# Attention and two MLPs on one core: the first stage in another order

## The chip, the core and the metric

The kernel runs on one core of a Trainium2 chip. The metric is the device time of one execution in microseconds (us), as a median of several. In the profile PE is TensorE's matmul, PEld its weight load, DVE is VectorE, ACT ScalarE, POOL GpSimd and SP the engine that issues most DMAs.

## What is computed

Inputs q, k, v have 4 batches, 8 heads, 576 positions and 64 columns per head. The attention is the sum of a pooled one (positions averaged by four, 144 of them, the result repeated four times) and a local one (each position sees those less than four away). Two MLPs follow on the 2304 tokens of 512 features, with 2048 inner features each:

```python
out_up = np.repeat(sm_attn(q_d, k_d, v_d), factor, axis=2)      # pooled by factor = 4
scores = np.where(np.abs(pos[:, None] - pos[None, :]) < factor, scale * q @ k^T, -1e9)
x = out_up + softmax(scores) @ v
h = x @ w_in;  x = (h - np.tanh(h)) @ w_out
h = x @ w_in2; x = (h * np.cos(h)) @ w_out2
```

## The kernel before

All MLP products are made of three products of operands split in a high and a low part (`xh`, `xl` and the like), so each weight tile of 128 inner features has to be split on the chip too. A weight tile goes through four steps of the class `Weights`: `load` (a DMA into one of two raw slots, in this stage), `begin` (two ScalarE instructions), `mid` (one on VectorE, then one cast, on GpSimd for the first three tiles and on ScalarE for the rest) and `end` (one subtraction on GpSimd). `tick` does a mid, a load, a begin and an end at once.

**First stage** (`first_attention`). The first 512 positions of batch 0 are handled on PE, as dense products. The stage is a list of steps, each with a key; the list is sorted by key and issued in that order. Every engine works through its own instructions in that order, and waits where an operand or a buffer isn't ready. So the keys set the order on each engine, and nothing else does. The steps:

- `load_nat`, `load_lo`, `load_vg`, `load_vl`, `load_vw`: loads of q and k by 128 positions, of the left-over 64 positions of the four batches, of v in pooled order, and of v in eight windows of 70 positions. All go through SP's queue. q, k and `vw` tiles share 12 buffers.
- `tr`, `tr_l`: transposes of a q or k tile on PE, copied out by ScalarE (q) or VectorE (k).
- `red_k`, `red_q`, `pooled_k`, `pooled_q`: sums by four; `pooled_q` also calls `left_q`, eight small GpSimd copies out of `klq`.
- `P.s`, `P.e`, `P.n`, `P.t`, `P.t2`, `P.v` for each of four head pairs: the pooled attention. Scores on PE and their maximum on VectorE, exponentials on ScalarE, the division on GpSimd, transposes on PE, value products on PE. `vsum` sums v by four on GpSimd for them.
- `b_s`, `b_m`, `b_n`, `b_t` for each of eight blocks of 64 positions: the local attention. Scores on PE (tile `cs`, three PSUM buffers), maximum and subtraction on VectorE and exponentials on ScalarE, the division on VectorE, transposes on PE copied by ScalarE (`cp`).
- `b_v`, `b_l` for each of four pairs of blocks: 32 value products on PE (`pa_o`), the addition of the pooled part on VectorE, the copy to `xh` on ScalarE; then `xl` by VectorE.

After each step of `tr`, `tr_l`, `b_s`, `b_t` and `b_v`, `at_time` puts one empty product on PE, `idle<-zero`, whose result is never read; `masks` puts ten at the start:

```python
def at_time(t, fn, *a):
    def run():
        fn(*a)
        if fn in with_pe:
            warm(1)
```

At keys from 26.5 on, `early` loads eight tiles of q, k and v for the first unit of the next part (1.7 MB), and from 27.19 on three ticks prepare the first weight tiles. Two raw slots are filled before, at 23.6.

**Then the planner** (`Plan`). The first MLP (`ffn1`, five chunks of tokens, four of them planned) runs on PE. Meanwhile GpSimd and VectorE do the local attention of the other batches in seven units of 128 rows: for each head a product `prod_s` or `prod_v` on GpSimd and a reduction on VectorE; three of the units also do the pooled attention of their batch on PE, for which `psum_qk` and `psum_v` sum by four on VectorE. A step has an engine, an assumed duration, a due time and what it waits for; the planner picks the order of all engines from these before the launch. A group of `ffn1` is 12 products per half into one of two PSUM buffers `h`, then tanh (ScalarE), subtraction (VectorE), copy `gh` (ScalarE) and `gl` (VectorE). The first two groups of chunk 0 are cut into token halves of 256, so that their first half can run before the last quarters of x exist. They have all their steps in the plan. After the planned part come the last chunk and the second MLP, which the change doesn't touch.

## Time and profile before

| | us |
|---|---|
| median of 3 runs (889.93 to 891.58) | 890.36 |
| the profiled execution's own time | 890.26 |
| its span, first to last instruction | 888.5 |
| PE busy | 871.6 |
| VectorE busy | 574.0 |
| ScalarE busy | 473.1 |
| GpSimd busy | 398.0 |

All times in the trace count from the first instruction. A row of the order of time gives start, length, engine, line and operation, and in brackets how long the engine stood idle before and what released it. Busy time of PE has all its products in it, the empty ones too. The first stage ends near 48 us.

### The profile page before, as it was taken

How to read it: one execution, taken by the hardware profiler on the slowest of the kernel's cores; microseconds unless marked ns; L12 is line 12 of the kernel's file. 1: busy time of each engine (PE TensorE's matmuls, PEld its weight loads, DVE VectorE, ACT ScalarE, POOL GpSimd, SP SyncE). 2: the span in 40 equal slices, each digit the busy share in tenths (PEclk: the TensorE clock that was granted, in tenths of full speed). 3: DMA queues.
4: the chain of work that ended last, by engine and by line, in shares of the span. 5: the costliest groups of instructions: out<-in, count | busy, mean ns of one | idle time of the engine just before them, and what ended most of it. 6: DMA issues, size and time to landing. Idle time of an engine off the chain costs nothing.

```text
span 888.5 us, 13043 instructions
## 1 busy us (share of the span) xinstructions
PE 871.6 (98%) x4648; PEld 722.9 (81%) x4648; DVE 574.0 (65%) x953; ACT 473.1 (53%) x967; POOL 398.0 (45%) x406
## 2 busy tenths in 40 slices
PE   8989999999999999999999999999999999999997
PEld 5677877998887888888888888888888888888896
DVE  5788978889988876554453676364546553655454
ACT  4778887354235432554674776354535543544454
POOL 7489999988978778410441232011101110111110
PEclk9999999999999999999999999999999999999999
DMA  9687745545434342532442131011001100000100
GB/s 213 202 266 264 252 154 175 179 128 161 137 106 130 103 152 81 185 111 95 142 143 72 72 102 41 0 48 48 1 1 47 48 1 24 24 25 1 36 13 24
DMA packets 72323, 89.03 MB, mean 100 GB/s; under 512 B 22720, under 2 KB 48326, under 8 KB 72258
## 3 DMA queue, kind: packets, MB, share of 16 engines
q1 hardware_dynamic: 70882, 83.22, 30.5%
q0 software_dynamic: 1232, 4.72, 1.6%
q8 instruction: 36, 0.59, 0.3%
q14 instruction: 29, 0.24, 0.1%
q10 hardware_dynamic: 144, 0.26, 0.1%
HBM read 78.74 MB, written 9.44 MB: 99 GB/s over the span
## 4 chain that ended last, share of the span: by engine, by line
PE 85%; POOL 5%; DMA 3%; issue 2%; ACT 2%; DVE 1%; SPq 1%; POOLq 0%; ACTq 0%; DVEq 0%
PE h L1082 39%; PE oacc L1354 22%; PE acc L1108 19%; POOL pr L869 2%; POOL pr L820 1%; DMA kt<-in_k_dram 1%; POOL i L251 1%; SPq L607 1%; POOL o L251 1%; PE pa_x L1019 1%; PE pa_s L491 1%; DMA lpt<-in_v_dram 1%; PE pa_t L525 0%; DMA raw<-in_moe_w_in_dram 0%; DMA raw<-in_moe_w_out_dram 0%
## 5 line engine op out<-in xcount | busy, mean ns | idle before, releaser
L1354 PE MATMUL oacc<-o,i 128*128 128x512 f32 x864 | 207.8, 390 | 0.0
L1082 PE MATMUL h<-xh,i 128*128 128x512 f32 (+1 forms) x656 | 197.4, 369 | 2.8 <-DVE gl L1131 2.2
L1369 POOL TENSOR_SCALAR y<-y 128x512 f32<-128x512 f32 (+1 forms) x80 | 46.0, 575 | 343.4 <-ACT y L1367 330.0
L1108 PE MATMUL acc<-gh,o 128*128 128x512 f32 (+1 forms) x640 | 194.3, 372 | 1.6 <-POOL o L251 1.6
L1082 PE MATMUL h<-x2h,i 128*128 128x512 f32 (+1 forms) x640 | 191.9, 368 | 0.0
L1354 PEld LDWEIGHTS oacc<-o,i 128*128 128x128 f32 x864 | 161.3, 188 | 33.2 <-ACT i L1095 0.4
L1082 PEld LDWEIGHTS h<-xh,i 128*128 128x128 f32 x656 | 118.6, 189 | 22.7 <-issue 3.0
L1108 PEld LDWEIGHTS acc<-gh,o 128*128 128x128 f32 x640 | 116.4, 189 | 22.7 <-POOL o L251 2.7
L1082 PEld LDWEIGHTS h<-x2h,i 128*128 128x128 f32 x640 | 117.0, 188 | 20.4
L820 POOL TENSOR_TENSOR pr<-qt,kt 128x896 f32<-128x896 f32 x56 | 118.8, 2132 | 14.8 <-DMA kt<-in_k_dram 6.9
L1082 PE MATMUL h<-xl,i 128*128 128x512 f32 (+1 forms) x328 | 119.4, 365 | 0.8 <-DVE xl L1034 0.4
L1108 PE MATMUL acc<-gl,o 128*128 128x512 f32 (+1 forms) x320 | 118.0, 369 | 0.0
L1082 PE MATMUL h<-x2l,i 128*128 128x512 f32 (+1 forms) x320 | 117.9, 368 | 0.0
L869 POOL TENSOR_TENSOR pr<-vt,s 128x896 f32<-128x896 f32 x56 | 105.8, 1945 | 9.5 <-DMA vt<-in_v_dram 4.8
L1374 DVE TENSOR_TENSOR h<-h,rr 128x512 f32<-128x512 f32 (+1 forms) x80 | 51.6, 645 | 80.5 <-ACT rr L1373 80.4
L1372 ACT ACTIVATE rr<-rr 128x512 f32<-128x512 f32 (+1 forms) x80 | 47.1, 588 | 98.3 <-DVE rr L1371 98.0
L1099 ACT ACTIVATE gh<-h 128x512 fp32r<-128x512 f32 x72 | 42.9, 596 | 75.5 <-PE acc L1108 50.1
L1376 DVE TENSOR_TENSOR i<-h,i 128x512 fp32r<-128x512 f32 (+1 forms) x80 | 50.7, 634 | 44.6 <-ACT i L1095 44.5
L1367 ACT ACTIVATE y<-h 128x512 f32<-128x512 f32 (+1 forms) x80 | 44.2, 552 | 60.0 <-PE h L1082 60.0
L1370 DVE TENSOR_TENSOR rr<-y,h 128x512 f32<-128x512 f32 (+1 forms) x80 | 50.3, 628 | 32.6 <-POOL y L1369 32.6
L1082 PEld LDWEIGHTS h<-xl,i 128*128 128x128 f32 x328 | 62.0, 189 | 10.2 <-DVE xl L1034 0.6
L825 DVE TENSOR_REDUCE s<-pr 128x14 f32<-128x896 f32 x56 | 60.3, 1078 | 14.4 <-POOL pr L820 14.2
(205 smaller groups left out, 1208.3 us busy)
## 6 DMA issues: line engine op xcount, KB each, us to landing
raw<-in_moe_w_in_dram SPq DMA_DIRECT2D x32, 512.0 KB, 6.5
raw<-in_moe_w_out_dram SPq DMA_DIRECT2D x32, 512.0 KB, 4.1
kt<-in_k_dram SPq DMA_DIRECT2D x48, 256.0 KB, 3.6
vt<-in_v_dram SPq DMA_DIRECT2D x48, 256.0 KB, 2.7
x2d<-xs SPq DMA_DIRECT2D x8, 512.0 KB, 2.9
x2l<-x2d POOLq DMA_DIRECT2D x4, 1024.0 KB, 5.6
out_dram<-os SPq DMA_DIRECT2D x15, 256.0 KB, 3.5
qt<-in_q_dram SPq DMA_DIRECT2D x24, 128.0 KB, 2.2
```

Source lines behind the costliest of these rows:

```text
L820: nc.gpsimd.tensor_tensor(out=pr.rearrange("p j f d -> p j (f d)"), in0=view(L["q", h], [[0, OFF], [1, 2 * D]], off=f * D), in1=view(L["k" ...
L825: nc.vector.tensor_reduce(out=L["s", u // 2][:, 2 * (u % 2) + e], in_=pr, axis=AX.X, op=ALU.add)
L869: nc.gpsimd.tensor_tensor(out=pr.rearrange("p f d j -> p j f d"), in0=view(L["v", h], [[D, OFF], [D, 2], [1, D]], off=f * D), in1=view(L[" ...
L1082: nc.tensor.matmul(hp[:, cs], lhsT=wt[:, kk * 128:(kk + 1) * 128], rhs=xt, start=(kk + c == 0), stop=(kk == KD - 1 and c == 2))
L1108: nc.tensor.matmul(acc[e], lhsT=wt[:, e * 128:(e + 1) * 128], rhs=gt, start=(f == 0 and i == 0), stop=(f == KF - 1 and i == 2))
L1354: nc.tensor.matmul(acc[t], lhsT=gt[:, t * 128:(t + 1) * 128], rhs=wt, start=(g == 0 and a_ == 0), stop=(g == KF - 1 and a_ == 2))
L1367: iy = nc.scalar.activation(y, hp, AF.Copy, scale=INV_TWO_PI, bias=ROUND)
L1369: ip = nc.gpsimd.tensor_scalar(out=y, in0=y, scalar1=-ROUND, scalar2=-TWO_PI_HI, op0=ALU.add, op1=ALU.mult)
L1370: nc.vector.tensor_tensor(out=r, in0=y, in1=hp, op=ALU.add)
L1372: nc.scalar.activation(r, r, AF.Abs)
L1374: nc.vector.tensor_tensor(out=hp, in0=hp, in1=r, op=ALU.mult)
L1376: nc.vector.tensor_tensor(out=G[f][1], in0=hp, in1=G[f][0].bitcast(F32), op=ALU.subtract)
```

## The change

The first stage has the same steps with other keys. An empty product follows a step only where its key is below 14. The three ticks are gone; load, begin, mid and end of the weights are steps of the stage with keys of their own. The first token halves of the first two MLP groups are steps too (`half`), and the plan takes these groups up at their second half. The eight early loads stand at 9.45 instead of 26.5. In the planned part ten products of the values are made by ScalarE (`prod_v_scalar`, 14 instructions each, `SCALAR` by unit and head), and the sums by four of seven entries are made by GpSimd with two additions, in place in the loaded tile (`sum_4`, `SUMS` by batch, kind and head; kind 0 has two sums, kind 1 one). The planner's constants and the engines' assumed first free times are other ones.

```diff
 
 
-LATENCY, SLACK, STICK = 0.08, 0.16, 0.17
+LATENCY, SLACK, STICK = 0.07, 0.16, 0.31
 
 
...
-                if fn in with_pe:
+                if fn in with_pe and t < WARM:
                     warm(1)
...
@@ -632,7 +652,24 @@
             G["vl"] = lo_load(v)
 
         def load_w():
-            W1.load(raw_a, 2)
+            W1.load(raw_a)
+
+        def begin_w():
+            assert W1.begun < W1.loaded
+            W1.begin()
+
+        def mid_w():
+            assert W1.mids < W1.begun
+            W1.mid()
+
+        def end_w():
+            assert W1.done < W1.mids
+            W1.end(nc.gpsimd)
+
+        def half(j):
+            assert W1.done > j and G["l", 0] and G["l", 1] and len(halves) == j
+            halves.append(group(ch, j, (j,), GS, False))
+            next(halves[j])
...
         with_pe = (tr, tr_l, b_s, b_t, b_v)
-        keyed = [(-9.08, masks), (-2.95, load_vl), (-1.21, load_vg), (13.94, pooled_k), (14.57, pooled_q), (23.6, load_w)]
+        keyed = [(-65.35, masks), (-0.93, load_vl), (4.13, load_vg), (12.99, pooled_k), (14.20, pooled_q)]
         for fn, nm, ts in (
-                (load_nat, "k", (-27.24, -17.23, -14.7, -18.39)),
-                (load_nat, "q", (-24.75, -9.9, -12.13, -14.48)),
-                (tr, "k", (-7.7, -9.06, -1.75, -9.05)),
-                (tr, "q", (-9.07, 12.44, 4.09, 7.14)),
-                (load_lo, "k", (-6.53, 7.68)),
-                (load_lo, "q", (-16.92, -1)),
-                (tr_l, "k", (13.83, 20)),
-                (tr_l, "q", (12.23, 25.24)),
+                (load_nat, "k", (-41.22, -26.44, -22.97, -34.25)),
+                (load_nat, "q", (-27.49, -14.70, -22.30, -19.81)),
+                (tr, "k", (-32.58, -17.04, 1.62, -33.53)),
+                (tr, "q", (-22.03, 8.94, 3.57, 4.78)),
+                (load_lo, "k", (-2.97, 6.88)),
+                (load_lo, "q", (-18.37, -1)),
+                (tr_l, "k", (10.88, 20)),
+                (tr_l, "q", (8.59, 16.86)),
         ):
             keyed += [(t, (fn, nm, i)) for i, t in enumerate(ts)]
         for fn, ts in (
-                (red_k, (3.96, 7.32, -1.37, 2.46)),
-                (red_q, (5.59, 12.45, 9.08, 8.75)),
-                (load_vw, (10.75, 7.88, 12.18, 3.99, -3.26, 8.66, 1.31, 0.91)),
-                (whole(P.s), (15.59, 16.13, 19.35, 18.35)),
-                (whole(P.e), (17.02, 18.39, 19.82, 19.23)),
-                (whole(P.n), (17.03, 18.4, 20.33, 21.49)),
-                (whole(P.t), (18.41, 21.2, 20.87, 25.75)),
-                (whole(P.t2), (19.25, 21.21, 23.95, 25.76)),
-                (whole(P.v), (20, 23.87, 27.22, 27.25)),
-                (b_s, (2.86, 14, 16.37, 16.46, 13.52, 20.14, 20.68, 19.06)),
-                (b_m, (12.2, 15, 17.07, 19.28, 13.53, 20.15, 23.21, 24.99)),
-                (b_n, (12.22, 17.81, 18.06, 19.36, 13.86, 20.16, 26.33, 25.07)),
-                (b_t, (13.87, 18.43, 19.97, 27.23, 17.92, 25.52, 28.49, 30.08)),
-                (b_v, (27.86, 28.36, 30.02, 31.66)),
-                (b_l, (31.35, 30.05, 30.42, 38.71)),
+                (red_k, (4.20, 8.14, 11.73, -7.26)),
+                (red_q, (-1.07, 11.04, 5.06, 9.35)),
+                (load_vw, (10.81, 2.62, 19.18, 8.20, 20.46, 22.38, 4.81, 17.90)),
+                (whole(P.s), (15.22, 15.48, 19.48, 17.29)),
+                (whole(P.e), (16.50, 17.34, 19.95, 18.80)),
+                (whole(P.n), (16.75, 17.40, 21.98, 19.76)),
+                (whole(P.t), (18.08, 20.01, 23.16, 20.48)),
+                (whole(P.t2), (18.94, 21.41, 24.52, 20.49)),
+                (whole(P.v), (20, 23.44, 25.49, 26.30)),
+                (b_s, (-10.60, 14, 16.51, 17.22, 5.89, 19.74, 20.17, 19.33)),
+                (b_m, (5.97, 15, 16.91, 19.12, 8.20, 22.99, 24.29, 20.71)),
+                (b_n, (9.30, 17.07, 18.48, 19.49, 10.42, 24.88, 27.74, 25.47)),
+                (b_t, (14.56, 19.45, 24.84, 26.21, 16.74, 27.43, 31.08, 31.66)),
+                (b_v, (28.50, 28.82, 36.30, 37.40)),
+                (b_l, (29.88, 34.47, 53.77, 56.00)),
         ):
             keyed += [(t, (fn, i)) for i, t in enumerate(ts)]
-        for nm, o_, ts in (("vg", vd, (17.17, 19.17, 20.37, 21.31)), ("vl", vl, (16.11, 20.3, 15.05, 14.86))):
+        for fn, ts in (
+                (load_w, (31.37, 7.62, 29.89, 10.27, 42.57)),
+                (begin_w, (24.69, 25.47, 30.70, 31.76)),
+                (mid_w, (26.53, 28.40, 36.10)),
+                (end_w, (26.60, 35.69)),
+        ):
+            keyed += [(t + 0.001 * i, fn) for i, t in enumerate(ts)]
+        keyed += [(t, (half, j)) for j, t in enumerate((36.45, 54.89))]
+        for nm, o_, ts in (("vg", vd, (16.95, 20.01, 21.04, 25.11)), ("vl", vl, (16.90, 22.74, 15.13, 26.28))):
             keyed += [(t, (vsum, o_, nm, u)) for u, t in enumerate(ts)]
         for t, fn in keyed:
             at_time(t, *(fn if isinstance(fn, tuple) else (fn,)))
         ch.x = None
...
+
+    def sum_cost(*a):
+        return ("POOL", 0.65) if a in SUMS else ("DVE", 0.56)
...
+        def prod_v_scalar(u, e):
+            h = 2 * u + e
+            if e == 0:
+                L["o", u] = ao.tile([128, 2, 2, D], F32, tag="o", name="o", bufs=10)
+            pr = at.tile([128, 2, D, OFF], F32, tag="pr", name="pr", bufs=2)
+            seen["v", u, e] = pr
+            s = L["s", u // 2].rearrange("p q j f -> p (q j f)")
+            for f in range(nf):
+                for j in range(OFF):
+                    i = ((2 * (u % 2) + e) * OFF + j) * nf + f
+                    nc.scalar.activation(pr[:, f, :, j], L["v", h][:, f + j, :], AF.Copy, scale=s[:, i:i + 1])
+                yield
+
...
+        def sum_4(o, t, off):
+            nc.gpsimd.tensor_tensor(out=t[:, off:off + 2, :], in0=t[:, off:off + 2, :], in1=t[:, off + 2:off + 4, :], op=ALU.add)
+            nc.gpsimd.tensor_tensor(out=o, in0=t[:, off, :], in1=t[:, off + 1, :], op=ALU.add)
...
+            if (b, 0, h) in SUMS:
+                sum_4(t[:, 0, e, :], L["q", h], 0)
+                yield
+                sum_4(t[:, 1, e, :], L["k", h], R - 1)
+                return
...
+                    if (ch.i, h) in SCALAR:
+                        p_ = plan.chain(prod_v_scalar(u, e), t, [("ACT", 0.8, dict(new=new, use=[name("v", h), s_, name("o", u)])),
+                                                                 ("ACT", 0.8, dict(use=[name("v", h), s_, pr, name("o", u)]))],
+                                        after=lds + out["soft", u // 2], prev=p_)[-1]
+                    else:
+                        p_ = plan.add("POOL", 1.97, t, lambda u=u, e=e: seen.__setitem__(("v", u, e), (prod_v(u, e, 0), L["prod"])[1]),
+                                      after=lds + out["soft", u // 2], prev=p_, new=new, use=[name("v", h), s_, name("o", u)])
...
-    TL = 26.5
-    HALVES, XLAST, RAWLAST = 2, 0.51, 3.90
-    TPGAP, TPS = 13.96, -2.17
-    REDLATE, LOADEARLY, FINEARLY, WLOAD = -6.92, 31.46, 7.92, 25.27
+    TL = 9.45
+    HALVES, XLAST, RAWLAST = 2, 5.76, 3.99
+    TPGAP, TPS = 14.11, -3.58
+    REDLATE, LOADEARLY, FINEARLY, WLOAD = -4.57, 13.51, 10.16, 18.40
     NORM = "A"
     WIDE = (), (2,), (2,), (2,)
-    WEARLY, URGENT = 50.47, 90.64
-    LENGTHS = 98.20, 59.66, 106.15, 108.05
-    SPANS = (-14.12, 71.46), (62.49, 107.38), (105., 143.), (157.39, 185.), (205.13, 257.46), (238.36, 274.93), (250.07, 330.89)
+    WEARLY, URGENT = 51.07, 123.07
+    LENGTHS = 98.26, 60.50, 113.62, 107.25
+    SPANS = (-14.69, 69.93), (71.07, 107.38), (105., 143.), (174.03, 185.), (215.87, 259.12), (236.67, 273.73), (257.96, 311.03)
     PRIO = 200
+    FREE = 1.18, 4.20, 4.00, 3.01
+    ACTV = "00000000010000000010010000011010000110011000000000000000"
+    SCALAR = [(i // 8, i % 8) for i, c in enumerate(ACTV) if c == "1"]
+    SUMBITS = "000000001000000001000000000000100000000010011001"
+    SUMS = [(1 + i // 16, i // 8 % 2, i % 8) for i, c in enumerate(SUMBITS) if c == "1"]
     AHEAD = 100.00
     LAG = 3
-    TE, TD, KE = 27.19, 1.82, 3
     NE, NG, NEARLY = 6, 3, 3
     rw = w2e = xb = W2 = None
     events = []
     exps = []
+    WARM = 14.00
+    halves, GS = [], {}
...
                     t = begin + 0.1 * j
-                c = plan.chain(group(ch, j, fs, G, j in WIDE[ci]), t, [
+                begun = ci == 0 and j < HALVES
+                c = plan.chain(halves[j] if begun else group(ch, j, fs, G, j in WIDE[ci]), t, [
                     ("PE", mm / 2, dict(new=[("ps_a" if j in WIDE[ci] else "ps_h", h)], use=[x], after=ready[:2 * per] + [wready.get(("i", f)) for f in fs])),
...
                 done[j] = c[-1]
-                firsts.append(c[1])
+                firsts.append(c[1 - begun])
...
-    events += [(TE + TD * i, 0, lambda: W1.tick(raw_a, nc.gpsimd)) for i in range(KE)]
...
-                dict(x=["x0"], raw=["raw3", "raw4"], wf=["wf1", "wf2", "wf3"]), dict(PE=0.0, ACT=0.5, DVE=1.5, POOL=1.0, SP=0.0))
+                dict(x=["x0"], ps_h=[f"h0.{j}" for j in range(HALVES)], raw=["raw3", "raw4"], wf=["wf1", "wf2", "wf3"]), dict(zip(("PE", "ACT", "DVE", "POOL"), FREE), SP=0.0))
```

By the new keys PE's steps come in this order: `tr` k 3, k 0, q 0, k 1; `b_s` 0; `tr` k 2, q 2, q 3; `b_s` 4; `tr_l` q 0; `tr` q 1; `tr_l` k 0; `b_s` 1; `b_t` 0; `P.s` 0, 1; `b_s` 2; `b_t` 4; `tr_l` q 1; `b_s` 3; `P.s` 3; `P.t` 0; `P.t2` 0; `b_s` 7; `b_t` 1; `P.s` 2; `b_s` 5; `tr_l` k 1; `P.v` 0; `P.t` 1; `b_s` 6; `P.t` 3; `P.t2` 3, 1; `P.t` 2; `P.v` 1; `P.t2` 2; `b_t` 2; `P.v` 2; `b_t` 3; `P.v` 3; `b_t` 5; `b_v` 0, 1; `b_t` 6, 7; `b_v` 2; `half` 0; `b_v` 3; `half` 1. SP's are: k 3 loads ahead of q 0, both left-over q loads and one of k, `vl`, `vw` 1, `vg`, `vw` 6, the last left-over k, one weight tile, `vw` 3, the eight early tiles, a second weight tile, `vw` 0, 7, 2, 4, 5, and the other three weight tiles as their slots come free.

## Rows read from the trace of the kernel before

**Rows 1.** The page: its head, and busy time with share and instructions of each engine.

```profile
span 888.5 us, 13043 instructions
...
PE 871.6 (98%) x4648; PEld 722.9 (81%) x4648; DVE 574.0 (65%) x953; ACT 473.1 (53%) x967; POOL 398.0 (45%) x406
```

**Rows 2.** Stretches: length, busy time per engine, PE's granted clock, DMA share, GB/s.

```profile
0.00:10.00 10.00, 7.68 (x35) 4.03 (x36) 2.31 (x4) 2.95 (x5) 8.12 (x31) 1.00 0.90 203
10.00:20.00 10.00, 9.72 (x103) 7.47 (x102) 8.59 (x22) 4.67 (x10) 5.38 (x17) 1.00 1.08 213
...
32.00:34.00 2.00, 1.80 (x16) 1.12 (x14) 1.38 (x5) 1.15 (x3) 1.92 (x4) 1.00 1.05 359
...
50.00:60.00 10.00, 7.80 (x54) 7.06 (x54) 9.98 (x15) 6.95 (x14) 9.86 (x8) 1.00 0.93 288
...
57.00:146.00 89.00, 86.39 (x416) 68.07 (x417) 76.22 (x130) 73.99 (x162) 85.69 (x69) 1.00 0.73 237
...
312.00:430.00 118.00, 118.00 (x530) 97.79 (x529) 68.05 (x102) 52.53 (x95) 53.91 (x42) 1.00 0.39 121
```

**Rows 3.** Waits of PE: who for whom, us in total, times, longest.

```profile
PE acc L1108 <- POOL o L251: 1.6, 2, 1.4
...
PE pa_s L491 <- POOL kT L479: 0.9, 1, 0.9
```

**Rows 4.** PE in order of time, first stage: start, length, instructions, idle before.

```profile
7.07 0.66 PE L667 MATMUL pa_tr<-ident,kg 128*128 128x128 f32 x4 [1.06 <-DMA kg<-in_k_dram]
...
16.80 0.38 PE L593 MATMUL idle<-zero 128*128 128x512 bf16 x1
17.02 0.28 PE L709 MATMUL cs<-mask_b,ident_b 128*128 128x280 bf16 x1
...
18.37 0.48 PE L388 MATMUL pa_s<-kd,qz 128*128 128x144 f32 x2
...
47.80 0.39 PE L593 MATMUL idle<-zero 128*128 128x512 bf16 x1
...
48.63 0.39 PE L1082 MATMUL h<-xl,i 128*128 128x256 f32 x1 [0.32 <-DVE xl L760]
...
54.25 0.28 PE L1082 MATMUL h<-xh,i 128*128 128x256 f32 x1
...
56.94 0.47 PE L1082 MATMUL h<-xh,i 128*128 128x512 f32 x1 [2.20 <-DVE gl L1131]
```

**Rows 5.** VectorE in order of time, first stage.

```profile
7.76 2.96 DVE L671 COPY kTn<-pa_tr 128x512 f32<-128x512 f32 x4 [6.56 <-PE pa_tr L667]
...
14.53 0.46 DVE L729 TENSOR_REDUCE cs<-cs 128x4 f32<-128x280 f32 x1 [0.46 <-ACT cs L722]
...
15.81 0.44 DVE L720 TENSOR_REDUCE cm<-cs 128x4 f32<-128x280 f32 x1
...
16.64 0.28 DVE L680 COPY klq<-pa_trl 128x128 f32<-128x128 f32 x1
```

**Rows 6.** GpSimd in order of time, first stage.

```profile
17.16 2.01 POOL L380 COPY qz<-klq 64x32 f32<-64x32 f32 x8
```

**Rows 7.** The tile of the value products: ns of one, shortest, median, longest.

```profile
L753 DVE TENSOR_TENSOR pa_o<-pa_o,up x4: 691/700/700, 41.9 to 48.5; 128x512 f32<-128x512 f32 x4
L756 ACT ACTIVATE xh<-pa_o x4: 585/597/597, 42.7 to 49.2; 128x512 fp32r<-128x512 f32 x4
L760 DVE TENSOR_TENSOR xl<-pa_o,xh x4: 680/688/692, 45.9 to 49.8; 128x512 fp32r<-128x512 f32 x4
```

**Rows 8.** SP's queue in order of time, first stage.

```profile
27.70 0.32 SPq L625 DMA_DIRECT2D vw<-in_v_dram  x1
```

**Rows 9.** Groups by line and shape: count, busy us, mean ns, idle before.

```profile
L869 POOL TENSOR_TENSOR pr<-vt,s 128x896 f32<-128x896 f32 x56 | 105.8, 1945 | 9.5 <-DMA vt<-in_v_dram 4.8 <-DVE o L873 3.5
...
L694 POOL TENSOR_TENSOR qd<-qh 128x128 f32<-128x128 f32 x4 | 1.6, 398 | 0.3
...
L555 ACT ACTIVATE up<-pa_v 128x128 f32<-128x128 f32 x12 | 3.3, 277 | 3.5 <-PE pa_v L552 3.5
```

More of the change, by code (lines that the diff above doesn't have):

```diff
@@ L560, in run @@
                 pass
+        run.__name__ = gen.__name__
         return run
     def first_attention(ch):
-        ev = []
+        ev, begun = [], set()
         NQ = 64
@@ L593, in warm, with before @@
                 nc.tensor.matmul(idle, lhsT=zero[:, 0:128], rhs=zero)
+        def before(fn, *a):
+            i = a[-1] if a else None
+            return {
+                "red_k": [("tr", "k", i)], "red_q": [("tr", "q", i)], "tr_l": [("masks",)],
+                "pooled_k": [("tr_l", "k", 0)], "pooled_q": [("red_q", t) for t in range(NT_)] + [("tr_l", "q", 0), ("masks",)],
+                "s": [("red_k", t) for t in range(NT_)] + [("pooled_k",), ("pooled_q",)],
+                "e": [("s", i)], "n": [("e", i)], "t": [("n", i)], "t2": [("t", i)],
+                "v": [("t2", i), ("vsum", "vg", i), ("vsum", "vl", i)],
+                "b_s": [("masks",)] + ([("tr", "q", i // 2)] + [("tr", "k", t) for t in range(NT_) if 128 * t < 64 * i + 67 and 128 * t + 128 > 64 * i - 3]
+                                       + [("tr_l", "k", 0)] * (i == NB - 1) if fn == "b_s" else []),
+                "b_m": [("b_s", i)], "b_n": [("b_m", i)], "b_t": [("b_n", i)],
+                "b_v": [(x, k_) for x in ("b_t", "load_vw") for k_ in (2 * i, 2 * i + 1)] + [("v", u) for u in range(NP)] if fn == "b_v" else [],
+                "b_l": [("b_v", i)], "half": [("b_l", 0), ("b_l", 1)],
+            }.get(fn, [])
         def at_time(t, fn, *a):
             def run():
+                step = (fn.__name__, *[x for x in a if isinstance(x, (int, str))])
+                assert all(x in begun for x in before(*step)), step
+                begun.add(step)
                 fn(*a)
-                if fn in with_pe:
+                if fn in with_pe and t < WARM:
                     warm(1)
@@ L976, in attention @@
                     t = t0 + (e + 0.5) * slot + 1.0
+                    lds = lds + [p_] if (b, int(w_[0] == "V"), h) in SUMS else lds
                     if w_[0] == "S":
                         out["qk", u] = plan.chain(psum_qk(u, e), t, [
-                            ("DVE", 0.61, dict(new=[("qkd", name("qkd", u))] if e == 0 else [], use=[name("q", h), name("qkd", u)], after=lds)),
-                            ("DVE", 0.61, dict(use=[name("k", h), name("qkd", u)], of=()))], after=lds, prev=out.get(("qk", u), [None])[-1])
+                            (*sum_cost(b, 0, h), dict(new=[("qkd", name("qkd", u))] if e == 0 else [], use=[name("q", h), name("qkd", u)], after=lds)),
+                            (*sum_cost(b, 0, h), dict(use=[name("k", h), name("qkd", u)], of=()))], after=lds, prev=out.get(("qk", u), [None])[-1])
                         out["qk2", u] = out.get(("qk2", u), []) + out["qk", u]
                     else:
-                        out["vd", u] = out.get(("vd", u), []) + [plan.add("DVE", 0.61, t, lambda u=u, e=e: psum_v(u, e), after=lds, prev=plan.last.get("vd"),
+                        out["vd", u] = out.get(("vd", u), []) + [plan.add(*sum_cost(b, 1, h), t, lambda u=u, e=e: psum_v(u, e), after=lds, prev=plan.last.get("vd"),
                                                  new=[("vd", name("vd", u))] if e == 0 else [], use=[name("v", h), name("vd", u)])]
@@ L1149, in ffn1 @@
         slots += [("s", j) for j in range(nu - 3, nu)]
-        G, acc, done, firsts = {}, [], {}, []
+        G, acc, done, firsts = GS if ci == 0 else {}, [], {}, []
         def second(j):
@@ L1215 @@
     W1, W2 = Weights(w_in1, w_out1), Weights(w_in2, w_out2)
-    units = [Unit(b, f0) for b in range(1, B) for f0 in (0, 2)] + [Unit(None, 0)]
+    units = [Unit(2 * b - 2 + f0 // 2, b, f0) for b in range(1, B) for f0 in (0, 2)] + [Unit(2 * B - 2, None, 0)]
     chunks = [Chunk([], 512)] + [Chunk(units[i:j], 256 * (j - i)) for i, j in ((0, 1), (1, 3), (3, 5), (5, 7))]
```

15 lines of the change are left out of this document (9 added, 6 removed).

## Prediction

> **What bounds the kernel now.** I read the page first: TensorE (PE) is busy for 871.6 of 888.5 us, VectorE 574.0, ScalarE 473.1, GpSimd 398.0 [rows 1]. The reader should see that only time in which PE stands still, or works on nothing, can be won. Next I cut the span into stretches [rows 2]. From 312 to 430 us PE is busy 118.00 of 118.00; nothing can be gained there. From 57 to 146 it lacks 2.61 us, from 50 to 60 alone 2.20, in the first ten 2.32. Last I read PE's own order of time in the first stage [rows 4], because busy time there hides something: after almost every step stands an empty product, `idle<-zero`, which counts as busy. The first stage has 32 of these beside the ten at its start (counted from `at_time` and `masks`). One costs PE 0.22 us from its start to the next start (16.80 to 17.02). So of the 56.94 us up to the first undisturbed MLP product some 7 are empty, and some 5 are waits (the page's gaps and those that hide behind an empty product). That stretch is where this change must earn or lose.
>
> **The change, part by part.** The profiled execution took 890.26 us, 1.76 more than its span and 0.10 below the median of the runs; the sum is made against 890.26.
>
> Empty products: only those of steps keyed before 14 stay (eight `tr`, `tr_l` of k 0 and q 0, `b_s` 0 and 4), 12 of 32. Twenty go: 20 x 0.22 = 4.4 us of PE. What this is worth depends on whether the next step is ready that much earlier, so I follow the stage in three legs.
>
> Leg 1, to the first pooled scores (`pa_s`, 18.37 [rows 4]). Before, PE did one `tr`, then stood 1.06 us for a key tile and did the other seven from 7.07 on. In the new order k 3, k 0 and q 0 are loaded and transposed first; I expect three done by about 7.2, with short waits for their copies. VectorE's copies, which began at 7.76, can then begin near 5.9. From there to the copy of `klq` at 16.64 its queue took 8.9 us [rows 5]. Now `b_n` of block 4 stands ahead of that copy too (1.3 us, as 14.53 to 15.81), one sum `red_k` (0.6) goes behind it, and some 0.3 of waits come on top: 5.9 + 9.9 = 15.8. Then come `red_k` 2 on VectorE and, beside it on GpSimd, `left_q`, 2.01 us for eight copies [rows 6], of which the first head pair needs two. The first scores start at about 16.8: 1.6 us sooner. Ahead of them PE will stand about 1 us, which the old order filled.
>
> Leg 2, first scores to the end of the last value product, `b_v` 3 (18.37 to 47.87, 29.5 us). Eighteen of the removed empty products lie here: -3.96. The first token half of MLP group 0 is put between `b_v` 2 and `b_v` 3: twelve products of 256 columns at 0.122 (48.63 to 54.25 in 46 steps), +1.46. Now the waits. Of those before, about 2.5 us lie in this leg. Following the queues by hand in the new order, with the durations of the same operations, I find new ones of like size: `b_s` 6 for the accumulator that `b_n` 3 frees (0.5), `P.v` 1 and 2 for ScalarE's copies (0.5 each), the two transposes before them for a PSUM buffer (0.3), the half group for `b_l` 1 (0.2), `b_v` 3 for the last copy behind a weight step on ScalarE (0.5). I take 2.5 against 2.5, bounds 1.5 and 5. The leg becomes 27.0, 2.5 us less, and the last value product ends near 43.8.
>
> Leg 3, from there to the first product of group 2 (47.87 to 56.94, 9.07). Before, four half groups followed, 48 products, then 2.20 us for `gl`. Now one half group is done already and the next fills part of the wait for the last quarter of x: add, copy and subtraction of 0.70, 0.60 and 0.69 [rows 7], with gaps 2.2 us, of which 1.46 is covered. Then the second half of group 0, 1.46, then tanh, subtraction, copy and subtraction. These four are as wide as the three, so about 2.9 with gaps; before, from the end of group 0 (34 steps after 48.63 and one drain, about 53.1) to 56.94 they took 3.9, with other work on VectorE between. 2.2 + 1.46 + (2.9 to 3.9) = 6.6 to 7.5; I take 7.0: 2.1 us less.
>
> Weight steps. Before, three ticks issued five loads, four begins, three mids, two ends; the new list issues the same numbers, in other places. They add no work. But two begins of 1.3 us each (two instructions as wide as those of [rows 7]) now stand on ScalarE ahead of `b_v` 2's copy, and each needs a raw slot that a mid frees; this is the last 0.5 of leg 2, at worst 2.
>
> Loads. The eight early tiles for the next unit (1.7 MB) and two weight tiles (0.5 MB each) move ahead of five of the `vw` tiles on SP's queue. The last `vw` was issued at 27.70 [rows 8]. At the 359 GB/s of 32 to 34 us [rows 2], 2.7 MB take 7.6 us, less what the queue idled before: these tiles land at about 33 to 37. `b_v` 0 comes to PE at about 36 by the legs, each further one 1.1 later. Hidden, but with little to spare; without this cover up to 2 us.
>
> Value products on ScalarE, sums on GpSimd. Ten products of 1.945 us leave GpSimd [rows 9]. Each becomes 14 ScalarE instructions of 128 x 64; the nearest row, 128 x 128, has 277 ns, and half of that is the lower bound: 2 to 3.9 us each. Seven entries are eight sums (one of q and k counts twice) that leave VectorE; GpSimd gains for each two short additions, 398 ns for 128 x 128 and less for 64, about 0.7 together, at most 0.8. From 57 to 146 GpSimd is busy 85.69 of 89 us, ScalarE 73.99 [rows 2]: the first is the fuller, and PE waits on it for weights and keys, 1.6 and 0.9 us [rows 3]. But only three of the products fall before the third chunk, against four sums: 5.8 - 2.8 = 3 us less GpSimd in about 150. Behind that PE is full anyway. Bounds on the waits after 57: 3 us fewer, 3 more; I take 0. The planner's other constants add no instruction; what they do to its order I can't read, and put within the same bounds.
>
> Sum: 890.26 - 1.6 - 2.5 - 2.1 = 884.1.
>
> The clock costs nothing in this sum. PE was granted 1.00 of full speed, the 2.4 GHz level, in every stretch here with work, even where it stood 2.20 us of ten or was busy 7.68 of ten [rows 2]. By my legs it works 26 of the 30 us from 14 to 44, no less, so I keep that level. The Trainium skill, TensorE: Matmul & The Clock Gate, A second HAM failure mode: psum-queue depth-cycling, speaks against it: many small pauses between groups of products, each for a PSUM buffer, can make the clock swing between its levels. This trace shows no swing, but also no long stretch of such pauses without empty products; by the page the sum would be nearer 897, the time of the third rival.
>
> **The rivals.** *The empty products filled time that is waited anyway.* Then the other queues set the pace of leg 2: VectorE, busy 8.59 of the ten us from 10 to 20, or the late `vw` tiles. For it: worked through without a break, VectorE's queue is only about 2 us ahead of PE. Against it: behind 13 of the 20 removed ones, from 16.80 to 47.80, the next step started within 0.25 us, so it was ready. Price: the 4.0 of leg 2, 888.1.
>
> *The gain is given back in the first MLP chunk.* PE arrives 6 us sooner and finds weights or keys missing. For it: GpSimd's full stretch and the waits on it. Against: weight steps and attention start sooner too, as all hang on the end of the same stage. Price: 2 to 6 us, so 886 to 890; taken at 889.
>
> *The clock falls*, the one that ends slower. Place: 14 to 44 us. At the 1.2 GHz level each of the 26 us of PE work takes twice as long. If that holds throughout, less some 4 us of waits that it covers, 906; it decides from 6 us of PE work at the lower level on, where the gain is gone. Taken at 897.
>
> **How the numbers follow.** The forecast, 884.1: 0.63, its own range 881 to 887 (waits of leg 2, leg 3, bounds after 57). Empty products without worth: 0.14. Given back: 0.14. Clock: 0.07. Anything else, either side: 0.02. Outside 880.5 to 889.5 lie the clock, a third of the case given back, and 0.06 for ends of the forecast: 0.18. A measurement tells 0.2%, 1.8 us, from no change, so faster means under 888.6. From the forecast 0.63, from the first rival 0.11, from the second 0.07: 0.81. The rest of these two, 0.10, is within the bound; the clock and the odd remainder, 0.09, are slower.
>
> **What would show it.** Right: the first `pa_s` near 16.8, the last value product ended near 44, the first 512-column product of group 2 near 50.8, and from there to the end the 831.6 us of before; each leg is one start in PE's order of time. Twenty rows of `idle<-zero` fewer, granted clock 1.00 throughout. Wrong: PE's `pa_o` waiting on the loads of `vw`, or waits in leg 2 above 5 us in all (first rival); PE's waits on GpSimd's `o`, `i` or `kT` after the stage grown by what the stage won (second); rows of the first stage at half clock (third).

## The result, and the profile after

The changed kernel took 903.01 us (median of 4 runs, 900.75 to 905.75), the kernel before 890.66 beside it (4 runs): a ratio of 1.0131, 95% interval 1.0114 to 1.0149. It is 12.4 us slower; 884.1 was forecast. The profiled execution took 905.75 us with a span of 904.0, against 888.5 [rows 1].

The head of the page and the busy times, which answer to [rows 1]:

```profile
span 904.0 us, 13133 instructions
...
PE 878.1 (97%) x4626; PEld 726.4 (80%) x4628; DVE 571.2 (63%) x945; ACT 503.9 (56%) x1107; POOL 385.9 (43%) x412
```

PE has 22 instructions fewer, all of them `idle<-zero` (20 rows instead of 42; the change takes out 20, so two are missing from the trace), and yet is busy 6.5 us longer. Work that takes longer with fewer instructions can be work at a lower clock, and the stretches show that it is. The stretches of [rows 2], and behind them a few chosen for the clock and one over the planned part (length, then busy us of PE, PEld, DVE, ACT, POOL, then the granted clock):

```profile
10.00:20.00 10.00, 9.68 (x104) 7.64 (x105) 8.72 (x22) 5.90 (x15) 6.82 (x18) 1.00 1.11 216
...
50.00:60.00 10.00, 6.20 (x15) 4.72 (x16) 7.97 (x12) 5.87 (x14) 7.60 (x6) 0.68 0.99 324
57.00:146.00 89.00, 86.47 (x411) 68.22 (x411) 72.64 (x123) 71.63 (x161) 81.18 (x66) 0.98 0.70 221
312.00:430.00 118.00, 115.49 (x553) 94.81 (x552) 70.50 (x109) 53.46 (x110) 56.46 (x44) 0.99 0.43 130
...
54.00:56.00 2.00, 1.58 (x4) 1.32 (x5) 2.00 (x4) 1.96 (x6) 2.00 (x2) 0.50 1.00 337
56.00:60.00 4.00, 4.00 (x11) 3.13 (x10) 1.97 (x3) 0.90 (x3) 1.60 (x3) 0.50 1.04 372
...
203.00:207.00 4.00, 4.00 (x24) 4.00 (x23) 2.56 (x3) 0.76 (x2) 2.28 (x2) 0.60 0.06 24
...
272.00:276.00 4.00, 4.00 (x14) 3.42 (x15) 3.29 (x6) 2.41 (x12) 0.38 (x1) 0.57 0.71 210
...
316.00:320.00 4.00, 3.59 (x14) 2.82 (x15) 3.78 (x6) 0.89 (x3) 2.00 (x2) 0.57 0.50 151
...
57.00:350.00 293.00, 280.98 (x1605) 233.13 (x1605) 232.54 (x385) 180.93 (x500) 232.76 (x200) 0.98 0.50 154
```

The last of these stretches in the kernel before:

```profile
57.00:350.00 293.00, 287.61 (x1669) 241.00 (x1670) 248.60 (x409) 154.60 (x370) 260.75 (x206) 1.00 0.52 163
```

Two things are to be seen. PE stands 12.0 us between 57 and 350 (293 - 280.98) instead of 5.4. And the clock is not 1.00 throughout any more: at 54 to 60, 203 to 207, 272 to 276 and 316 to 320 it was granted 0.50 to 0.60, the 1.2 GHz level for most of the stretch. Length times what is missing from 1.00 gives 1.0 + 2.0 + 1.6 + 1.7 + 1.7 = 8.0 us.

PE in order of time in the first stage answers to [rows 4] (start, length, instructions, idle before):

```profile
17.23 1.77 PE L388 MATMUL pa_s<-kd,qz 128*128 128x144 f32 x12 [0.21 <-POOL qz L380]
...
43.38 1.17 PE L787 MATMUL pa_o<-cp,vw 70*64 70x64 f32 x32 [1.20 <-ACT cp L777]
44.48 0.39 PE L1169 MATMUL h<-xh,i 128*128 128x256 f32 x1
...
50.54 0.30 PE L973 MATMUL pa_qk<-ident,qkd 128*128 128x128 f32 x1 [0.70 <-DVE qkd L957]
53.14 0.33 PE L973 MATMUL pa_qk<-ident,qkd 128*128 128x128 f32 x1 [2.30 <-DVE qkd L959]
54.42 0.77 PE L1169 MATMUL h<-xh,i 128*128 128x512 f32 x1 [0.96 <-DVE gl L1218]
```

Up to the last value product the new stage does what was forecast: first scores at 17.23 (16.8), the last value product over at 44.48 (43.8; 47.87 before). Then it loses: 9.94 us to the first product of group 2 instead of 7.0, with 3.96 us of waits of which the longest, 2.30, is for a k sum of the next unit. The products behind it run at half clock.

PE's waits of 2 us and more, which answer to [rows 3] (1.4 was the longest there, and 2.20 in [rows 4]; each line gives us in total, times, longest):

```profile
PE pa_v L550 <- DVE xl L1115: 2.5, 1, 2.5
PE pa_qk L973 <- DVE qkd L959: 2.3, 1, 2.3
PE pa_s L491 <- POOL kT L479: 2.1, 1, 2.1
PE pa_t L525 <- DVE xl L1115: 2.1, 1, 2.1
```

The other three stand at 316.4, 271.9 and 202.5, right ahead of the three later stretches at the low clock. What stands ahead of the one at 316.4, on ScalarE, then on VectorE:

```profile
311.11 1.85 ACT L931 ACTIVATE pr<-vt,s 128x64 f32<-128x64 f32 x7 [2.37 <-issue]
312.80 0.59 ACT L1212 ACTIVATE th<-h 128x512 f32<-128x512 f32 x1
313.30 1.82 ACT L931 ACTIVATE pr<-vt,s 128x64 f32<-128x64 f32 x7
314.96 0.58 ACT L1113 ACTIVATE xh<-pa_x 128x512 fp32r<-128x512 f32 x1
```

```profile
313.42 0.70 DVE L1214 TENSOR_TENSOR h<-h,th 128x512 f32<-128x512 f32 x1 [1.59 <-ACT th L1212]
...
315.57 0.69 DVE L1115 TENSOR_TENSOR xl<-pa_x,xh 128x512 fp32r<-128x512 f32 x1 [1.12 <-ACT xh L1113]
```

The tanh (`th`), whose products on PE had ended by 310.3, stands behind one block of seven moved products and the copy `xh` behind the next; VectorE waits for each, and PE for VectorE's `xl`. The stall at 202.5 has the same shape: seven products from 196.62, `th` at 198.62, and VectorE 1.68 us idle for it. The one at 271.9 has no such block ahead: there GpSimd's copy to `kT` stands behind two products of its own.

From the first product of group 2 to the end PE took 18.0 us more than before (849.6 against 831.6, each span less 54.42 and 56.94). Summed over the trace, its idle time there grew from 5.4 to 13.2 us and 8.1 us went to the clock; the remaining 2.1 no row singles out.

### The profile page after: what moved, and what is told of

Its sections match the earlier page's. It is cut to its first block, busy times and chain, and to the rows that moved or that the text cites. A ratio compares the mean times of both kernels' runs of the same rounds, so it can differ in the third digit from the quotient of the medians.

```text
span 904.0 us, 13133 instructions
## 1 busy us (share of the span) xinstructions
PE 878.1 (97%) x4626; PEld 726.4 (80%) x4628; DVE 571.2 (63%) x945; ACT 503.9 (56%) x1107; POOL 385.9 (43%) x412
## 4 chain that ended last, share of the span: by engine, by line
PE 62%; ACT 1%; DMA 1%; DVE 1%; issue 0%; ACTq 0%
PE h L1169 30%; PE oacc L1441 22%; PE acc L1195 9%; DMA raw<-in_moe_w_out_dram 0%; ACT pr L931 0%; DMA raw<-in_moe_w_in_dram 0%; PE pa_x L1100 0%; DVE wf L235 0%; ACT gh L1186 0%; ACT wf L225 0%; ACT raw L227 0%; ACT o L244 0%; ACT th L1399 0%; DVE xl L1115 0%; DVE gl L1402 0%
## 5 line engine op out<-in xcount | busy, mean ns | idle before, releaser
L1169 PE MATMUL h<-xh,i 128*128 128x512 f32 (+1 forms) x656 | 200.0, 373 | 2.2 <-DVE gl L1218 2.0
L1195 PE MATMUL acc<-gh,o 128*128 128x512 f32 (+1 forms) x640 | 197.3, 376 | 2.6 <-ACT gh L1186 1.6
L1169 PEld LDWEIGHTS h<-xh,i 128*128 128x128 f32 x656 | 120.5, 191 | 23.3 <-POOL i L251 1.7
L1195 PEld LDWEIGHTS acc<-gh,o 128*128 128x128 f32 x640 | 118.5, 192 | 25.0 <-ACT gh L1186 2.5
L918 POOL TENSOR_TENSOR pr<-vt,s 128x896 f32<-128x896 f32 x46 | 87.3, 1936 | 24.7 <-DVE o L935 16.7
L1195 PEld LDWEIGHTS acc<-gl,o 128*128 128x128 f32 x320 | 61.6, 192 | 11.3 <-DVE gl L1402 1.1
```

The lines of the kernel that those rows point to most:

```text
L918: nc.gpsimd.tensor_tensor(out=pr.rearrange("p f d j -> p j f d"), in0=view(L["v", h], [[D, OFF], [D, 2], [1, D]], off=f * D), in1=view(L[" ...
L1169: nc.tensor.matmul(hp[:, cs], lhsT=wt[:, kk * 128:(kk + 1) * 128], rhs=xt, start=(kk + c == 0), stop=(kk == KD - 1 and c == 2))
L1195: nc.tensor.matmul(acc[e], lhsT=wt[:, e * 128:(e + 1) * 128], rhs=gt, start=(f == 0 and i == 0), stop=(f == KF - 1 and i == 2))
```

## The experiments

All times are medians beside the kernel before on the same chip, all ratios against it. **The offset** is by how much later the same MLP product starts in one trace than in another (negative: sooner); products are counted in units of 512 columns.

**1. The first stage alone.** The changed kernel with both lists empty and the planner's constants of before; what is left is the stage, its new order and its empty products.

```
-    SCALAR = [...]          +    SCALAR = []
-    SUMS = [...]            +    SUMS = []
-LATENCY, SLACK, STICK = 0.07, 0.16, 0.31
+LATENCY, SLACK, STICK = 0.08, 0.16, 0.17
...
```

> Only the new first stage (keys, fewer empty products, weight steps and half groups in it, the engines' first free times), with the planner's constants of before and without products on ScalarE and sums on GpSimd. Theory of the prediction (the stage itself is worth 6 us and the rest of the change lost it): 883 to 887. Theory S: 884 to 890, as the wait for the keys of the first unit behind group 1 may stay with its stretch of half clock, 3 to 4 us. If the stage itself is what makes the later part late: 895 or more.

888.31 us, ratio 0.9962 (0.9947 to 0.9977): faster, by 3.1 of the 6.2 us forecast for it. The offset against the kernel before is -2.0 to -2.2 from product 432 to the end, so nothing that the stage wins is lost later. Its own losses, first in PE's order of time, then in the stretch behind it:

```profile
37.19 2.79 PE L787 MATMUL pa_o<-cp,vw 70*64 70x64 f32 x64 [1.65 <-DMA vw<-in_v_dram]
```

```profile
39.00:46.00 7.00, 7.00 (x67) 6.21 (x68) 3.98 (x6) 5.56 (x12) 3.59 (x4) 0.51 0.47 148
```

A `vw` tile is late by 1.65 us, and the 7 us behind it run at 0.51. So the price named for uncovered loads ("up to 2 us") was paid, and 3.4 us of clock with it.

**2. Neither move, the changed planner constants.** Only the two lists are emptied.

> The change without products on ScalarE and without sums on GpSimd; the new first stage and the planner's other constants stay. Theory S: as without the products alone, 887 to 894. Theory G: clearly below the kernel that keeps the sums, by 5 or more. Theory P: still 900 or more.

889.65 us, 0.9988 (0.9972 to 1.0004). That is 1.3 us more than experiment 1, which the intervals do not separate: the constants cost little or nothing. The other 13 or so of the changed kernel are the two moves and what they do to the planner's order.

**3. The products left on GpSimd, the sums moved.** `SCALAR = []` alone.

> The change with all value products back on GpSimd; sums on GpSimd, keys and constants stay. Theory S (a product on ScalarE holds its in-order queue for two blocks of 1.7 us, planned as 0.8 each, so that copies which PE waits for come late, and PE's stalls of over 2 us are followed by half clock): the stalls between 180 and 330 us go, with them three stretches of half clock; 903 falls by 9 to 14, to 889 to 894. Theory P (the planner's other constants order the attention steps badly, whoever makes the products): 900 or more. Theory G (the sums on GpSimd make keys and values late): 900 or more.

903.68 us, 1.0131 (1.0113 to 1.0148). The theory that ScalarE's products alone cost the time fell here: without them nothing is won, in the order that the planner then makes.

**4. The products at the cost that they have.** In the trace after, one block of seven products takes 1.85 us and ScalarE's next step starts 1.7 us after its first; the planner reckoned with 0.8.

```
-   ("ACT", 0.8, ...), ("ACT", 0.8, ...)
+   ("ACT", 1.73, ...), ("ACT", 1.73, ...)
```

> The change with one number other: the planner takes a block of seven ScalarE instructions as 1.73 us, as measured, and not as 0.8; the same work on the same engines. Theory S with the wrong cost as its core: the planner then puts the blocks where they hold nothing up, and most of 9 to 14 us comes back, 890 to 896. If ScalarE simply has no room for the work: no gain, 900 or more. Theory P: 900 or more.

896.20 us, 1.0042 (1.0029 to 1.0056). The wrong cost is worth about 7 us, half of what the moves lose.

**5. and 6. Each move alone at its true cost.** Products at 1.73 a block without the sums; sums at 0.85 a pair (0.65 before) without the products.

> The changed kernel without the sums on GpSimd and with the planner told what a block of seven products on ScalarE takes (1.73 us instead of 0.8): of the two moves only the ten value products on ScalarE remain. With neither move the kernel took 889.65, with both at this cost 896.20. If the products are what the 6.5 us come from: 894 to 896. If the sums are: 889 to 891. If they only hurt together, or the planner's order decides it case by case: in between, 891 to 894.

> The changed kernel without the products on ScalarE, and the planner told what a pair of short sums takes on GpSimd (0.85 us instead of 0.65). The other corner of the square: neither move 889.65 us, both 896.20, products alone 902.55, sums alone at the wrong cost 903.68. If each move delays the attention that must end before an MLP chunk can begin (the loss of 8 to 9 us between the products 576 and 624 in all three), 896 to 904 with the loss there again. If it was the wrong cost, as it was for the products (6.8 us), 890 to 897.

902.55 us (1.0133, 1.0110 to 1.0156) and 901.85 us (1.0129, 1.0114 to 1.0144). Each alone is worse than both, so the planner's order, which each small change of a cost makes anew, carries much of it. What such an order loses, in PE's order of time, first with neither move, then with the products alone (rows of `acc` and `h` between these left out):

```profile
201.05 0.60 PE L525 MATMUL pa_t<-ident,pe 128*128 128x128 f32 x4
...
206.34 0.36 PE L1195 MATMUL acc<-gh,o 128*128 128x256 f32 x1
...
209.30 0.38 PE L525 MATMUL pa_t<-ident,pe 128*128 128x128 f32 x2
...
211.01 0.29 PE L540 MATMUL pa_v<-pe,vd 128*64 128x16 f32 x4
```

```profile
208.80 0.49 PE L1169 MATMUL h<-xh,i 128*128 128x512 f32 x1 [0.98 <-ACT xh L1113]
...
214.74 0.45 PE L487 MATMUL pa_s<-kT,ql 128*32 128x144 f32 x8 [0.70 <-DVE xl L1115]
...
217.53 0.50 PE L1169 MATMUL h<-xh,i 128*128 128x512 f32 x1 [1.05 <-ACT xh L1113]
...
222.48 0.30 PE L540 MATMUL pa_v<-pe,vd 128*64 128x16 f32 x4
```

With neither move the second products of the MLP chunk (`acc`) last until 209.3, between the last steps of the attention, and `pa_v` of the leftover scores follows at 211.0. With the products moved `acc` is over at 206.0, the attention ends 11.5 us later at 222.5, and PE has nothing to put between: it waits, a microsecond at a time, for x of the next chunk. Between products 576 and 624 the offset against neither move goes from -2.6 to +7.4; in these 22.2 us PE stands 4.1, the half clock from 218.8 to 222.2 takes 1.7, and the rest is products of the attention that lie elsewhere in the other order. The changed kernel itself loses only part of its time here: its offset against neither move goes from 2.8 to 5.5, then to 12.1 at product 816, behind the stall at 271.9, and to 16.5 at 1104. In the run with sums alone the loss comes later (from +2.3 at product 960 to +12.5 at 1104, 3.4 of it half clock). GpSimd's list of waits between 280 and 350 us is headed there by late values; that PE's loss hangs on them is not shown:

```profile
POOL pr L918 <- DMA vt<-in_v_dram: 10.1, 3, 6.2
```

**7. and 8. The same moves without a new order.** The kernel of experiment 2, planned as if nothing had moved, and then at the planned places the ten products given to ScalarE (7), or the eight sums to GpSimd (8). In the eighth the sums overwrite rows of k, q and v that a later product reads, so its output is another; its instructions are whole. In the seventh both blocks of a product stand together, fourteen instructions, at a place that was picked for GpSimd.

```
-   lambda u=u, e=e: seen.__setitem__(("v", u, e), (prod_v(u, e, 0), ...))
+   lambda u=u, e=e: list(prod_v_scalar(u, e)) if (ch.i, 2 * u + e) in MOVED else ...
...
-   if (b, 0, h) in SUMS:
+   if (b, 0, h) in MOVED:
```

> The kernel with neither move (889.65 us), its order on each engine kept as planned for value products on GpSimd, but the ten products handed to ScalarE at their places. It takes the planner's new order out of the question. If the order costs the time, and not the work: 888 to 891. If the work does (a product takes 3.6 us and more on ScalarE instead of 1.92 on GpSimd, ahead of copies that the next chunk waits for): 893 to 903.

> The kernel with neither move (889.65 us), its order on each engine kept as planned with all sums on VectorE, but the seven entries' sums (eight sums, sixteen short additions) handed to GpSimd at their places. As for the products (910.31 in that way), this takes the planner's new order out. If the moved work itself delays GpSimd, which is the fuller engine from 57 us on: 8 x 0.85 = 6.8 us more on it, of which at least the part behind which a chunk waits shows: 892 to 898. If the 12 us of sums_true come from its order (loads of vt that GpSimd waits for up to 6.2 us): 888.5 to 891.

910.31 us (1.0218, 1.0201 to 1.0235) and 892.88 us (1.0022, 1.0005 to 1.0039), against 889.65. Here the two part. The sums cost 2 to 4 us at the planned places (the offset against neither move is +2.1 from product 816 to 1600, and 1.4 at the end), so most of the 12 us of experiment 6 is its order. The products cost 21 us at the planned places: from the first product of group 2 to product 1104 PE stands 17.2 us instead of 4.1, and 9.6 instead of 1.7 go to the clock. A planner that knows of the blocks can put them elsewhere, so this is the price of the block where it hurts, not of the work as such. In the trace of experiment 7 (ScalarE in order of time, then PE):

```profile
305.43 3.50 ACT L931 ACTIVATE pr<-vt,s 128x64 f32<-128x64 f32 x14
308.78 0.36 ACT L505 ACTIVATE pe<-pa_s,pm 128x144 f32<-128x144 f32 x1
...
309.55 3.50 ACT L931 ACTIVATE pr<-vt,s 128x64 f32<-128x64 f32 x14
312.89 0.71 ACT L517 ACTIVATE pe<-pe,pr__4011 128x144 f32<-128x144 f32 x2
```

```profile
313.35 1.21 PE L525 MATMUL pa_t<-ident,pe 128*128 128x128 f32 x4 [4.71 <-ACT pe L517]
```

Fourteen small instructions stand ahead of the softmax steps of the pooled scores on an in-order queue, and PE waits 4.71 us for the step behind them. ScalarE is far from full there (31.2 of 52 us from 260 to 312): it is the place in the queue that costs, not the share of busy time.

**9. All empty products back.** Experiment 1 with `WARM = 1e9`.

> The new first stage alone, as in first_only (888.31 us there), with an empty product again behind every step of it (20 more, 0.22 us each on TensorE). Theory A, the stalls of about 2 us become half-clock stretches because nothing covers them: the stretches at 39.0 and 56.0 us (3.4 us each and more, about half of it lost, so some 4 to 5 us together) go or shrink, and the 20 products cost up to 4.4 us, of which what lies in waits is free: 886 to 889. Theory B, the empties are only work: the time grows by 2 to 4.4 us, 890 to 893, and the half-clock stretches stay.

888.86 us, 0.9972 (0.9958 to 0.9985), the same as without them within the intervals. The wait for `vw` is gone and the stretch from 39 to 46 is at 1.00 again; the one from 54 on at half clock stays, 6.8 us long instead of 3.4. Twenty empty products more neither cost nor win: part of what they take (4.4 us) comes back by that wait (1.65) and by the clock (5.1 us lost to it in the trace of experiment 1, 3.4 here).

**10. The early loads late.** Experiment 1 with the eight loads of the next unit behind the `vw` loads again.

```
-    TL = 9.45
+    TL = 23.5
```

> first_only with the eight early loads of the next unit put behind the loads of vw on the SP queue, as late as before. If the wait of 1.65 us at 37.19 for a vw tile comes from these loads, it goes, and with it the half-clock stretch of 39.0 to 45.8 us (3.4 us lost): 883.5 to 886.5, unless the wait at 54.44 for the k sum grows. If the vw tile was late for another reason, or the clock fell for another reason, the time stays within 0.6 us of first_only (888.3).

888.16 us, 0.9964 (0.9951 to 0.9977): no change in the time, but not for want of effect. The wait and the half clock at 39 are gone, and product 0 starts at 40.10 instead of 43.67. Then PE waits 2.30 us for the k sum, half clock follows, and at 214 a second stretch at half clock takes 1.6 more; the offset falls from -3.9 to -2.3 there.

**11. and 12. The planner told the true times of the stage,** with the loads early (11) and late (12):

```
-    HALVES, XLAST, RAWLAST = 2, 5.76, 3.99
+    HALVES, XLAST, RAWLAST = 2, 5.76, 7.00
-    FREE = 1.18, 4.20, 4.00, 3.01
+    FREE = 1.18, 4.20, 7.20, 3.01
```

> first_only with the planner told the times of the new first stage as measured: VectorE free 3.2 us later (7.20 instead of 4.00) and the raw weight tile there at 7.00 instead of 3.99. The planner then puts the first transposition of the k sum behind group 2's products on TensorE. If this in-order queue cost leg 3 its gain: the wait of 1.78 us at 54.44 goes, and the half-clock stretch behind it (3.4 us long, 1.7 lost): 885 to 887. If VectorE is simply the slower engine there, group 2 waits for gl instead, and the time stays within 0.6 us of 888.3.

> first_late and first_times together: early loads late, and the planner told when VectorE and the raw tile are there. Up to product 48 first_late had won 0.8 us against the kernel before, first_times had lost 0.1 with the half clock from 39.2 on. If VectorE's k sums and subtractions ahead of gl set the start of group 2, it comes sooner here, as they stand behind: product 48 at 59 to 61 us. The time hangs on what the planner does with the rest: 884 to 887 if it is as good as first_late's, 890 to 893 if the loss of 5 us between products 288 and 624 of first_times comes again.

892.73 us (1.0019, 1.0004 to 1.0034) and 889.75 us (0.9994, 0.9981 to 1.0007). The planner moved the transposition of the k sum behind group 2, as expected, and PE waited for `gl` instead: 2.94 us in 11, 3.15 in 12. In 12 group 2 starts at 52.37 instead of 54.06 in experiment 10, and leg 3 is 8.52 us instead of 9.96, so VectorE's k sums ahead of `gl` do cost some 1.4 us. The rest of leg 3's excess, 1.5, stands among VectorE's other work and is not taken apart; and the planner's new order loses later on (the offset against the kernel before goes from -3.0 at product 48 to -0.9 at the end).

**13. A filler in the stall.** Experiment 10 with 26 empty products of 256 columns ahead of the two `pa_qk`.

```
             a = ps_a.tile([128, 2, 128], F32, tag="a", name="pa_qk")
+            if ch.i == 0 and u == 0:
+                for _ in range(26):
+                    nc.tensor.matmul(a..., lhsT=W1.hi["i", 0][:, 0:128], rhs=chunks[0].x[0][:, 0, 0:256])
```

> first_late (888.16 us) with 26 empty products of 256 columns (3.1 us) on TensorE ahead of the first two pa_qk, in the place of the waits of 0.71, 2.30 and 0.95 us that stand there. If the stall makes the clock fall, the half-clock stretch of 3.4 us at 53.9 goes: product 48 starts some 1.3 to 1.7 us sooner (60.0 to 60.4 instead of 61.69), and the time is 886.4 to 887, less still if the stretch at 214.4 goes too. If the clock falls for another reason, the stretch stays and the time is 888 to 889.

885.40 us, 0.9946 (0.9931 to 0.9960): 5.4 us under the kernel before, the fastest of all. PE in order of time, then two stretches of this kernel, then the same two of experiment 10:

```profile
48.64 3.29 PE L974 MATMUL pa_qk<-xh,i 128*128 128x256 f32 x26
51.76 0.57 PE L976 MATMUL pa_qk<-ident,qkd 128*128 128x128 f32 x2
53.29 0.47 PE L1172 MATMUL h<-xh,i 128*128 128x512 f32 x1 [0.96 <-POOL i L251]
```

```profile
54.00:56.00 2.00, 2.00 (x10) 1.61 (x10) 2.00 (x5) 1.65 (x4) 1.41 (x2) 1.00 0.94 340
...
214.00:218.00 4.00, 4.00 (x19) 3.31 (x18) 3.98 (x8) 1.89 (x5) 3.61 (x8) 1.00 0.42 134
```

```profile
54.00:56.00 2.00, 1.94 (x5) 1.58 (x6) 2.00 (x3) 1.93 (x6) 1.95 (x2) 0.50 1.05 388
...
214.00:218.00 4.00, 4.00 (x12) 3.12 (x11) 3.89 (x8) 1.44 (x3) 3.78 (x6) 0.57 0.67 197
```

The same two microseconds hold ten products instead of five. The filler is work without use in a place where PE would have stood, and the clock stays: the traces of all the other kernels with the new stage, thirteen, show half clock that begins between 50.9 and 56.7 us, this one none. Product 48 starts at 59.38 instead of 61.69; 0.77 of these 2.31 us were there already at the first product of group 2 (53.29 instead of 54.06), ahead of the half clock. The later stretch went too, though the steps around it are the same. The mean granted clock was 0.997 to 1.000 in the four executions, 0.994 to 0.996 in the five of experiment 10.

## Why the prediction was wrong

**Leg 1** held: first scores at 17.23 against 16.8, VectorE's copies from 6.30 on (5.9 forecast), `klq` out at 16.41 (15.8).

**Leg 2** held in its size (27.25 us against 27.0, ended at 44.48 against 43.8), though not in its parts: of the 2.5 us of waits PE stood 1.52, and 1.20 of these at `b_v` 3, where 0.5 was forecast. Nor did the cover hold that it assumed. "Hidden, but with little to spare" was right for the changed kernel and wrong for the same stage in experiment 1, where the tile came 1.65 us late; and once it was hidden for good (experiment 10), product 0 came 3.6 us earlier than in experiment 1.

**Leg 3** failed as a size: 9.94 instead of 7.0. "With other work on VectorE between" was seen as a reason for 3.9 instead of 2.9; it is more. VectorE's k sums, a weight step and a sum of scores stand ahead of `gl`, and one weight step took 2.13 us instead of 0.69, beside a product on GpSimd. PE, in order, stood behind the k sums' transposition as well.

**"Bounds on the waits after 57: 3 us fewer, 3 more; I take 0"** is the step that failed, together with its reason, that a product moved from a full engine to one with room is a gain. It was sized by busy time, and busy time did move as meant: from 57 to 350 GpSimd is busy 232.76 us instead of 260.75, ScalarE 180.93 instead of 154.60. The waits grew all the same, from 5.4 to 12.0 us, and half clock came behind them. The price per product was inside its bounds (two blocks of 1.8 us against "2 to 3.9"); what was missing is that each stands as a block in an in-order queue ahead of tanh, copies and softmax steps that the next steps wait for. The trace after shows this at two of its three new stalls, experiment 7 at places not planned for it. Experiments 2 to 8 put the moves at 6.5 to 14 us with the planner's order and at 21 for the products in the old order. How much of the changed kernel's loss is the blocks and how much the order is open: without the products, in yet another order, it lost as much (experiment 3). That "behind that PE is full anyway" was read from a trace in which the attention ends in time; where it ended 11.5 us later (experiment 5), PE was not.

**"The planner's other constants ... within the same bounds"** held: 1.3 us at most.

**"The clock costs nothing in this sum"** failed. About 8 of the 18.0 us lost from group 2 on are half clock, 3.0 of them right behind leg 3. The third rival had the mechanism and the wrong place: not through the first stage from 14 to 44 by many small pauses, but behind single stalls of 2 us and more. The moves made three new ones; the first, of 2.30 us, is there without them too (experiment 2). Experiment 13 shows it for the first: with the stall filled the half clock is gone. For the other three it was not tried. The second rival, gain given back, had the direction right and the size (889) and place wrong: not weights or keys in the first chunk, but waits at 202 to 316 us, two on the steps that make x of a next chunk (`xl`) and one on keys (`kT`, 2.1 us).

**The empty products**: 4.4 us removed was taken to be worth about 4 in leg 2. Experiment 9 shows that beside these stalls they are worth nothing, as the first rival had it. Only with the loads late, the stall filled and neither move made (experiment 13) does the kernel gain 5.4 us. That this is close to the 6.2 forecast for the stage is luck: there the first product of group 2 starts at 53.29, 3.65 us sooner than before, not at 50.8; the rest was won later.

## What to carry to other kernels

Price a move to another engine by its longest block and by what stands behind that block in the queue, at the place where a stage ends; the busy share of the engine did not show it here. When a planner lays out queues from costs, measure the costs first, and compare whole orders: the right price of one block changed the time by some 7 us here, and moving one thing less made it worse by 6. A stall on TensorE can cost twice, once as time and once as half clock behind it; in the one place where it was tried, products without use cost less than the stall.

## What the runs showed of the hardware

**The clock falls behind a short stall.** In the trace after, waits of 2.06 to 2.51 us at four places were each followed by 1.6 to 3 us lost at the 1.2 GHz level, and in experiment 1 a wait of 1.65 by 3.4. A wait is not enough to tell: before, PE waited 2.20 us ahead of group 2 [rows 4] with the clock at 1.00; in experiment 3 it waited 1.92 and 1.71 us at 341.6 and 346.1, at 1.00 too; and in experiment 10 the clock fell at 214 behind waits of 0.37 and 0.70 us among short products, and with the same steps 1 us earlier (experiment 13) it did not. The clock also differs between executions of one kernel, whose instructions keep their order: the ten of experiment 8 took 890.80 to 895.89 us, the shortest at a mean granted clock of 0.997, the longest at 0.989. What decides between these is open.

**A weight step on VectorE beside GpSimd.** The step that combines a weight tile in SBUF (`wf`, 128 x 512) took 0.69 us at 42.88 and 2.13 at 46.69 in the trace after, the second beside a product of GpSimd's. VectorE in order of time:

```profile
42.88 0.69 DVE L235 SCALAR_TENSOR_TENSOR wf<-wf,raw 128x512 uint32<-128x512 uint32 x1 [2.33 <-ACT raw L227]
...
46.69 2.13 DVE L235 SCALAR_TENSOR_TENSOR wf<-wf,raw 128x512 uint32<-128x512 uint32 x1
```

The Trainium skill, GPSIMD Engine Reference, 8. Key points, states that the two engines share their interfaces to SBUF and contend when VectorE's instruction has two inputs there; the rows agree.

**Small ScalarE instructions.** Seven of 128 x 64 with a scale per partition took 1.85 us, one 402 ns in the middle of 140, so (1850 - 402) / 6 = 241 ns from start to start. Fourteen are 3.4 us where the planner had 1.6. By the Trainium skill, ScalarE: Activation LUTs, What ACT_TABLE_LOAD costs, which gives 186 ns and 0.833 ns for each element, 93 ns more for a scale per partition and 93 less back to back, an estimate is 186 + 93 + 0.833 x 64 - 93 = 239 ns; the row agrees.
